# A recurrent attention kernel on one core: float32 rows per segment in DRAM, earlier loads of the first side operands, an order of waits, and a new order of units

## The chip, the core and the metric

The kernel runs on one core of one Trainium2 chip. The metric is the device time of one execution in microseconds. PE is TensorE, DVE VectorE, ACT ScalarE, POOL GpSimd, and SP (SyncE) is the queue from which nearly all DMAs are issued.

## The reference

Two attention branches read the same 2048 x 512 input; a gate mixes them row by row. Cut to what matters:

```python
# branch A: 32 heads of 128; 64 segments of 32 rows; a memory of M = 8 rows
mem = mem0
for s in range(64):
    h = concatenate([mem, x[32 * s:32 * (s + 1)]])        # 40 rows
    q, k, v = h @ Wq, h @ Wk, h @ Wv                      # per head
    p = softmax(where(mask, q @ k.T * E ** -0.5, -1e9))   # memory rows see all, the others are causal
    o = sum_over_heads(p @ v @ Wo)
    mem, out[s] = o[:8], o[8:]                            # the memory goes into the next segment
# branch B: 32 heads of 16; 4 blocks of 512 rows; softmax inside a block, and a running sum
for s in range(4):
    o = sig(beta) * (phi(q) @ Mem) / (phi(q) @ z + 1e-6) + (1 - sig(beta)) * softmax(q @ k.T * D ** -0.5 + mask) @ v
    Mem, z = Mem + phi(k).T @ v, z + sum(phi(k))
b = o @ wo
g = sigmoid((x * gate_w).sum(-1))
return g * a + (1 - g) * b
```

Branch A is a recurrence: segment s + 1 can't begin its products before the eight memory rows of segment s are there.

## The kernel before, in words

**How it is built.** The kernel records operations engine by engine (`Prog`, L79), with what each reads and writes, and then emits each engine's list in the recorded order. `_plan_waits` (L153) decides for which earlier operations each one waits on a semaphore: its dependencies are sorted by age, the youngest first, and those that an earlier wait covers are dropped. `emit` (L192) issues the waits that are left in the list's order. Where an instruction has two, the built program keeps the first of the list on the instruction, and the second becomes an instruction of its own ahead of it.

**Prologue.** 256 KB pieces of x and branch B's weights, then Wk, Wq and Wv in 1 MB pieces and Wo, are loaded while PE projects the first three blocks of branch B (`b_projections`, L650, a list of 52 pieces). Their Q, K and V go to DRAM (`scr_kqd`, `scr_vd`), and `BAttn.load` (L879) brings what one job of branch B's attention needs back: K in four loads of 16 KB for each half G (`KTj`), Q in one of 128 KB (`QTj`), V in one (`Vj`). `build` (L239) asks for the first job's operands after pieces 36 (K, G = 0), 37 (Q), 38 (K, G = 1), 40 and 42 (V).

**The order.** All the rest is cut into units, and `A_ORDER` (L1049) is a written-out list of their names, in which they are recorded. It sets the order on every engine. A `~` behind a name swaps ACT and DVE for the PSUM copies of that unit. Units of segment s:

- `s.K0x s.K0y s.K1x ... s.V1y`: half passes of the projections of the segment's 32 columns (8 of memory, 24 of x), PE, L1266; `Q1x`, `Q1y` are quarters by head, L1492. `k0`, `q0`, `v0` ... copy them out of PSUM (ACT or DVE; those of V are called `Vev`), `TK0`, `TQ0` ... transpose them on DVE.
- `Z` (mask bias), `S` (scores), `X` (exp, ACT), `Y` (mask), `M` (sums), `L` (reciprocal, ACT), `N`, `n` (normalise: DVE, POOL), for two halves of the heads.
- `PV` (values, L1616), `E0` to `E3` (copies to `OT_sb`), `W0` to `W3` (output projection, L1353), `hm` (the memory of the next segment: a transpose, a copy and two additions on DVE, L1653 to L1658, the additions named `hma`, `hmb`, into `xTp`).
- `H` copies the segment's float32 result to `WN` (one buffer of 128 x 256, ACT or DVE), and `ws` stores it to DRAM (`sta`). `H` of the next segment waits until that store has read `WN`.

The last 8 rows of each segment feed no memory. Those of four segments are taken together as a group (`L0.` to `L15.`: projections; `O0.` to `O15.`: their output projection, of which `e` copies to the same `WN`, `olev`, and `s` stores it, `sto`). `T0.` to `T15.` finish a group of 128 rows: `l` loads the float32 rows, `a` adds their two halves on POOL (`asum`), `b` is branch B's output projection, `t` scales that on ACT into `t1_sb` (`t1`, L1453, after `asum` has read that tile), `f` mixes on DVE and stores the output. The last segment's rows go straight from PSUM to the output (`finz`, L1662), with a part `t1z` (ACT, L1458) that stands behind `t1` of group 15.

`bS`, `bE`, `bP`, `bT` are branch B's scores (L923), exponentials (ACT, L944, with a mask on POOL, L950), values (L976) and the rest; `pj`, `pp` project its last block late; `wl` loads a piece of Wo.

**The rows in DRAM.** `scr_aRow` is `[16, 4, 4, 5, 8, 256]`: group, column quarter, segment in the group, 8-row part, row, columns. A segment stores parts 0 to 3 of its place, the left rows part 4 of all four segments. A group's load reads parts 1 to 4 in four DMAs of 128 KB, two into `aF` and two into `t1_sb`:

```python
rows[0:SEG * n, q, :]  <-  aRow[g, 2 * i + q, 0:n, 1:5].rearrange("r o i w -> r (o i) w")   # i, q in 0..1; n = 4, 3 in the last group
```

Each load depends on all of the group's stores. `aF` lives through the whole program; `t1_sb` lies where the prologue's buffers were.

Of the kernel before, what the change touches and what calls it, by code (L numbers as in the profile page):

```python
# [78 lines left out]
class Prog:  # L79
# [73 lines left out]
    def _plan_waits(self):  # L153
# [5 lines left out]
        top = {}  # L159
# [8 lines left out]
        for o in sorted((o for e in self.ENGS for o in self.ops[e] if o.born is not None), key=lambda o: o.born):  # L168
# [70 lines left out]
def build(nc, es, A_x, A_mem0, A_Wq, A_Wk, A_Wv, A_Wo, B_wq, B_wk, B_wv, B_wo, B_beta, gate_w, out, dbg=None):  # L239
# [31 lines left out]
    def alloc(stack, *specs):  # L271
        at, spans = 0, {}
        for name, shape, dt, n in specs:
# [21 lines left out]
          ("WN", [128, 256], F32, 0), ("tt", [128, 2 * C, SEG], F32, 0), ("tu", [128, 2 * C, M], F32, 0), ("aF", [128, DM], F32, 0))  # L295
# [16 lines left out]
          ("oTt", [128, 16, 32], F32, 0), ("t1_sb", [128, DM], F32, 0))  # L312
# [13 lines left out]
    dram("aRow", [NG, 4, 4, 5, 8, 256], F32)  # L326
# [4 lines left out]
    def Rs(name):  # L331
        if name not in R:
            R[name] = Res(name)
            home = v.home(name)
            if home:
# [6 lines left out]
             ("OT", "OT_sb"), ("oTt", "oTt"), ("t1_", "t1_sb"))  # L342
# [47 lines left out]
    for n in range(len(pieces)):  # L390
# [15 lines left out]
        if n in (36, 37, 38, 40, 42):  # L406
            bat.load(0, n // 2 % 2 if n != 37 else 0, "kv"[n // 40] if n != 37 else "q")
# [371 lines left out]
class LateB:  # L779


    def __init__(self, v):
# [4 lines left out]
        self.vst = v.t1_sb[:, :].bitcast(BF16)[:, 0:544].rearrange("p (h w) -> p h w", w=17)  # L787
# [71 lines left out]
class BAttn:  # L859
# [190 lines left out]
    L0.xl 0.Q1x 0.q1x L0.KL1x L0.QL1x bS L0.KL1y bE bE pj L0.KL0x wl pj wl L0.VL0x L0.KL1e~ L0.VL0y L0.VL1x wl pp~ L0.VL0e L0.VL1y L0.VL1e~ 0.TQ1x 0.K0x  # L1050
    0.K0y L0.KL0y 0.K1x L0.QL1y 0.Q1y 0.q1y 0.V0x L0.KL0e~ 0.k0 0.K1y 0.V0y L0.QL0x 0.Q0x L0.QL0y wl pj L0.QL1e 0.TK0 wl pj bE wl 0.Q0y wl L1.xl 0.k1
    0.V1x 0.v0~ 0.q0~ 0.Z1 L0.QL0e~ 0.TK1 0.TQ0 L1.KL0x L1.QL0x 0.qt bE 0.TQ1y L1.KL1x 0.S1 0.S0 L1.KL1y 0.V1y 0.X1 0.X0 0.Y0 L1.KL1e~ 0.M1 L1.KL0y
    L1.QL0y 0.M0 L1.QL1x L1.QL1y L0.VLt pj 0.v1 wl 0.L0 0.N0 0.n0 pp 0.L1 L1.QL1e 1.qt 0.N1 pj bP 0.n1 L1.KL0e~ 0.PV 0.E1 bP 0.E0 0.W0 0.W1 0.E3 0.E2 0.W2
    0.W3 0.hm bS pp 1.Z1 bE L1.QL0e 1.K0x bE 1.Q0x 1.Q1x 1.q1x~ 1.Q0y 0.H bE 1.q0 1.TQ1x 1.K0y 1.Q1y 1.TQ0 1.K1x 0.oL bE 1.K1y 1.k0 1.q1y bP bP 1.k1 1.TK0
    1.S0 1.X0 bS 1.TQ1y 0.ws bE 1.V0x 1.TK1 bE 1.S1 1.Y0 1.V0y 1.M0 1.V1x 1.X1 1.L0 1.M1 1.V1y 1.v0 1.L1 1.n0 1.n1 pj pj 1.N0 1.N1 1.v1~ 1.PV bE pp~ 1.E2~
    1.E0 1.E1~ L1.VL0x 1.W0 1.E3~ bE 1.oL 1.W1 1.W2 1.W3 bP 1.hm 1.H bP bS L1.VL0y bE bE 2.K0x bT 2.K0y L1.VL0e 2.Q0x 2.Q1x bE bE 2.Q0y 2.q1x 2.qt 2.k0~
    2.Q1y 2.TK0 bP bP bS 2.q0~ 2.TQ0 2.q1y~ 2.K1x 2.TQ1y bE 2.K1y bE 2.S0 bE 2.V0x 2.X0 1.ws pj 2.TQ1x pj 2.k1~ bE 2.TK1 2.Z1 2.S1 2.Y0 2.M0 2.V0y bP 2.X1
    2.L0 bP 2.M1 bS pp~ 2.L1 2.V1x 2.n0 2.v0 2.N1 bE 2.N0 2.V1y 2.n1 bE 2.v1 pj bE pj bE 2.PV 2.E0 2.E3 pj 2.E1~ pj 2.W0 2.W1 bT 2.E2 2.W2 bP 2.W3 bP bS
    pp 2.hm bE bE pj pj bE 3.K0x 3.qt 2.H 3.K0y 3.Q0x 3.Q0y 3.k0~ 3.TK0 3.q0~ 3.K1x 3.K1y pp~ 3.Q1y bE 3.TQ0 3.k1 3.q1y~ 3.Z1 3.Q1x 3.S0 3.TK1 3.TQ1y
    3.V1x 3.V1y 3.q1x 3.TQ1x 3.S1 3.X0 3.Y0 2.ws pp 3.M0 3.X1 bS 3.M1 bP 3.L0 3.v1 bP 3.n0 3.V0x 3.V0y L1.VL1x 3.L1 2.oL 3.n1 3.N0 bE bE 3.N1 3.v0 bE  # L1060
    L1.VL1y 3.PV pj 3.E0~ 3.E1~ pj 3.E3 bE L1.VL1e 4.qt 3.W0 3.W1 bP 3.E2 3.W2 bT 3.W3 bS pp bP 3.hm 3.H bE bE 3.oL pj pj 4.Q1x 4.K0x L1.VLt pp bT 4.K0y
# [24 lines left out]
    L4.KL1e~ 13.Q0x 13.Q0y 13.K1x 13.q0~ 13.k0~ 13.K1y 13.TK0 13.TQ0 13.Q1x 13.Q1y 13.k1 13.q1x 13.S0 13.TK1 13.q1y 13.TQ1x 13.V1x 13.V1y 13.TQ1y 13.X0
# [149 lines left out]
def plan_a(v, nseg):  # L1236
# [136 lines left out]
    def ol_units(g):  # L1373
# [96 lines left out]
    def segment(s):  # L1470
# [201 lines left out]
        def w_rows():  # L1672
            rows_out(v.aRow[g, :, r, 0:4], WN[:, :], [rw], Rs("aTd%d" % s), P.group("as%d" % s, "as%d" % (s % 2)), "sta%d" % s)
# [90 lines left out]
```

## Time and profile before

| | us |
|---|---|
| runs: median (lowest, highest) of 3 | 854.94 (851.87, 856.57) |
| profiled execution | 855.72 |
| its span, first to last instruction | 852.7 |
| PE busy | 791.9 (93%) |
| DVE busy | 581.7 (68%) |
| ACT busy | 567.4 (67%) |
| POOL busy | 287.6 (34%) |
| granted PE clock | 0.992 |

The span is what the rows of the trace add up to; 3.0 us of the profiled execution lie outside of it. In rows that say who waited for whom, the numbers are the total in us, how often, and the longest. In rows of the timeline they are the start and the length in us, and in brackets how long the engine had been idle and what ended that. A busy PE is not PE at its peak, since the ends of pipelined products are modelled.

### The profile page before, as it was taken

How to read it: one execution, taken by the hardware profiler on the slowest of the kernel's cores; microseconds unless marked ns; L12 is line 12 of the kernel's file. 1: busy time of each engine (PE TensorE's matmuls, PEld its weight loads, DVE VectorE, ACT ScalarE, POOL GpSimd, SP SyncE). 2: the span in 40 equal slices, each digit the busy share in tenths (PEclk: the TensorE clock that was granted, in tenths of full speed). 3: DMA queues.
4: the chain of work that ended last, by engine and by line, in shares of the span. 5: the costliest groups of instructions: out<-in, count | busy, mean ns of one | idle time of the engine just before them, and what ended most of it. 6: DMA issues, size and time to landing. Idle time of an engine off the chain costs nothing.

```text
span 852.7 us, 51641 instructions
## 1 busy us (share of the span) xinstructions
PE 791.9 (93%) x23291; PEld 490.6 (58%) x23291; DVE 581.7 (68%) x1467; ACT 567.4 (67%) x1370; POOL 287.6 (34%) x728
## 2 busy tenths in 40 slices
PE   9978999999998999999999899999999999999883
PEld 4535556565565656655666566556656555655552
DVE  4535666766778776787778686777776577787543
ACT  5535777866767677776747677686576776885442
POOL 4501333432424333342422334252242342452120
PEclk9989999999999999999999999999999999999998
DMA  9995332122212211212213121112222121211221
GB/s 331 416 364 165 81 100 73 33 64 64 70 41 74 51 56 52 61 41 63 79 30 81 38 67 55 48 44 54 68 73 60 48 58 58 58 32 37 78 81 44
DMA packets 98867, 72.33 MB, mean 85 GB/s; under 512 B 56304, under 2 KB 92760, under 8 KB 97112
## 3 DMA queue, kind: packets, MB, share of 16 engines
q1 hardware_dynamic: 97928, 68.24, 26.7%
q8 instruction: 182, 2.98, 1.5%
q10 hardware_dynamic: 720, 0.80, 0.3%
q14 instruction: 37, 0.30, 0.1%
HBM read 43.43 MB, written 25.58 MB: 81 GB/s over the span
## 4 chain that ended last, share of the span: by engine, by line
PE 68%; DMA 10%; DVE 8%; ACT 6%; issue 3%; POOL 2%; SPq 2%; POOLq 0%; DVEq 0%; ACTq 0%
PE ps L1266 35%; PE ps L1353 12%; PE ps L1492 5%; DMA scr_aRow<-WN 5%; PE ps L1616 2%; PE ps L923 2%; PE ps L976 2%; POOL PT L950 2%; DMA t_sb<-scr_aRow 2%; DMA scr_kqd<-stgk 2%; PE ps L1552 1%; PE ps L1585 1%; DMA QTj<-scr_kqd 1%; ACT R_sb L1595 1%; PE ps L827 1%
## 5 line engine op out<-in xcount | busy, mean ns | idle before, releaser
L944 ACT ACTIVATE PT<-ps 128x512 bf16<-128x512 f32 x320 | 173.5, 602 | 57.2 <-PE ps L923 48.8
L950 POOL TENSOR_SCALAR_AFFINE_SELECT PT<-PT 128x128 bf16<-128x128 bf16 (+2 forms) x320 | 121.1, 378 | 219.1 <-ACT PT L944 200.2
L1266 PE MATMUL ps<-Wv_sb,xTp 128*32 128x512 bf16 x2048 | 144.0, 379 | 3.9 <-ACT WN L374 3.0
L1266 PE MATMUL ps<-Wk_sb,xTp 128*32 128x512 bf16 x2048 | 134.8, 380 | 6.7 <-DVE xTp L1658 2.9
L1353 PE MATMUL ps<-Wo_sb,OT_sb 128*32 128x256 bf16 x4032 | 123.2, 273 | 7.8 <-issue 4.7
L1353 PEld LDWEIGHTS ps<-Wo_sb,OT_sb 128*32 128x32 bf16 x4032 | 102.4, 97 | 29.3 <-ACT OT_sb L374 19.7
L1604 POOL TENSOR_TENSOR P_sb<-P_sb,R_sb 128x64 bf16<-128x64 bf16 x128 | 47.4, 370 | 163.1 <-ACT R_sb L1595 159.9
L1266 PEld LDWEIGHTS ps<-Wk_sb,xTp 128*32 128x32 bf16 x2048 | 56.9, 96 | 58.8 <-ACT PT L944 5.6
L374 ACT ACTIVATE OT_sb<-ps 128x320 bf16<-128x320 f32 x176 | 65.2, 438 | 32.8 <-PE ps L1627 32.2
L374 ACT ACTIVATE QN_sb<-ps 128x256 bf16<-128x256 f32 (+1 forms) x156 | 68.5, 442 | 27.5 <-PE ps L1266 20.9
L374 ACT ACTIVATE KN_sb<-ps 128x512 bf16<-128x512 f32 x97 | 58.1, 600 | 41.7 <-PE ps L1266 40.9
L1266 PE MATMUL ps<-Wq_sb,xTp 128*32 128x512 bf16 x1024 | 71.7, 380 | 3.5 <-DVE xTp L1658 3.2
L1278 DVE STREAM_TRANSPOSE KT_sb<-KN_sb 128x256 f32<-128x256 f32 x128 | 55.7, 436 | 26.9 <-ACT KN_sb L374 24.0
L1278 DVE STREAM_TRANSPOSE QT_sb<-QN_sb 128x128 f32<-128x128 f32 (+1 forms) x192 | 63.4, 337 | 14.2 <-ACT QN_sb L374 12.1
L1492 PE MATMUL ps<-Wq_sb,xTp 128*32 128x256 bf16 x2048 | 71.9, 273 | 0.0
L376 DVE CAST V_sb<-ps 128x512 bf16<-128x512 f32 x83 | 56.9, 688 | 19.6 <-PE ps L1266 17.9
L1653 DVE STREAM_TRANSPOSE tt<-ps 128x256 f32<-128x256 f32 x63 | 28.3, 450 | 56.1 <-PE ps L1353 55.5
L1492 PEld LDWEIGHTS ps<-Wq_sb,xTp 128*32 128x32 bf16 x2048 | 56.5, 97 | 15.9 <-DVE QN_sb L376 0.4
L1566 ACT ACTIVATE P_sb<-ps 128x224 bf16<-128x224 f32 x128 | 45.5, 358 | 29.1 <-PE ps L1557 23.9
L376 DVE CAST OT_sb<-ps 128x320 bf16<-128x320 f32 x80 | 36.5, 486 | 26.6 <-PE ps L1627 26.4
L1266 PEld LDWEIGHTS ps<-Wv_sb,xTp 128*32 128x32 bf16 x2048 | 44.0, 95 | 16.5 <-ACT WN L374 3.7
L1599 DVE TENSOR_TENSOR P_sb<-P_sb,R_sb 128x160 bf16<-128x160 bf16 x128 | 41.5, 336 | 16.1 <-ACT R_sb L1595 15.3
(142 smaller groups left out, 1408.6 us busy)
## 6 DMA issues: line engine op xcount, KB each, us to landing
scr_aRow<-WN SPq DMA_DIRECT2D x79, 128.0 KB, 2.3
Wk_sb<-in_A_Wk_dram SPq DMA_DIRECT2D x4, 1024.0 KB, 9.7
Wq_sb<-in_A_Wq_dram SPq DMA_DIRECT2D x4, 1024.0 KB, 13.6
Wv_sb<-in_A_Wv_dram SPq DMA_DIRECT2D x4, 1024.0 KB, 16.2
Wo_sb<-in_A_Wo_dram SPq DMA_DIRECT2D x8, 512.0 KB, 6.4
scr_vld<-VNL SPq DMA_DIRECT2D x16, 256.0 KB, 2.8
VL<-scr_vld SPq DMA_DIRECT2D x64, 64.0 KB
aF<-scr_aRow SPq DMA_DIRECT2D x30, 128.0 KB
```

The lines of the kernel that those rows point to most:

```text
L374: P.op("act", lambda a: a.activation(dst, src, ACT.Copy), reads=[v.rbank[k] for k in bks], writes=dres, name=name)
L376: P.op("dve", lambda d: d.tensor_copy(dst, src), reads=[v.rbank[k] for k in bks], writes=dres, name=name)
L944: P.op("act", lambda a: a.activation(pt, v.pb[bk], ACT.Exp, scale=v.SCALE_B), reads=[v.rbank[bk]], writes=[rp], name="be%d_%d" % (n, t))
L950: P.op("gp", lambda g: g.affine_select(mv, mv, [[0, len(cut)], [1, 128]], ALU.is_ge, 0.0, base=0, channel_multiplier=-1), reads=[rp], writ ...
L1266: ins = pe.matmul(pb[bk][SEG * j:SEG * (j + 1), :], lhs(c), cols(w, j) if split else w[:, 512 * j:512 * (j + 1)], start=(c == 0), stop=(c ...
L1278: P.op("dve", lambda d: d.transpose(to, src), reads=reads, writes=writes, name=name)
L1353: ins = pe.matmul(pb[bk][SEG * j:SEG * (j + 1), 0:256], lhs(h), Wo_sb[:, h, :].rearrange("p (k q c) -> p q k c", q=2, c=64)[:, j % 2], sta ...
L1492: ins = pe.matmul(pb[bk][SEG * j:SEG * (j + 1), 0:256], lhs(c), cols(w_sb[:, c, 2048 * b + 1024 * half:2048 * b + 1024 * (half + 1)], j), ...
L1566: P.op("act", lambda a: a.activation(P_sb[:, b, :], pb[bk][:, 0:So], ACT.Exp, scale=SCALE), reads=[rbank[bk]], writes=[Rs("Pm%d" % b), Rs( ...
L1599: P.op("dve", lambda d: d.tensor_tensor(wide[b][:, :, 0:L], wide[b][:, :, 0:L], R_sb[:, b, :].rearrange("p (i q) -> p i q", q=L), ALU.mult ...
L1604: P.op(ENG["n"], lambda d: d.tensor_tensor(left, left, grp04(R_sb[:, b, :]), ALU.mult), reads=[Rs("R0_%d" % b)], writes=[Rs("PL%d" % b)], ...
L1653: P.op("dve", lambda d: d.transpose(v.tt[:, :, :].rearrange("p (k n) t -> p k n t", n=2), src), reads=[rbank[wb["bk"]]], writes=[Rs("tt")] ...
```

## The change

1. The DRAM rows are stored per segment, `aTd [64, 128, 256]`, and per group of left rows, `aTl [16, 128, 256]`. A store is the 128 x 256 tile as it is. A group's load becomes eight DMAs (six in the last group): for each segment one of 24 partitions x 4 x 1 KB and one of 8 partitions x 4 x 1 KB. Each depends on its own store alone, and all share one semaphore ring.
2. `aF` and `t1_sb` become one tile `AR [128, 2, 512]`, in the place of `t1_sb`.
3. The first job's K and Q of branch B are asked for after pieces 30, 31 and 32 instead of 36, 37 and 38; V stays.
4. Each operation's waits are sorted once more: on PE first those for operations named `hm...` and `Vev...`, last an engine's wait for itself.
5. `A_ORDER` is a new list of the same units, with the `~` marks set anew. On ACT there are 10 copies more and on DVE 10 fewer.

```diff
@@ _plan_waits
+            o.waits.sort(key=lambda d: 2 if d.eng == o.eng else 0 if o.eng == "pe" and d.name.startswith(("hm", "Vev")) else 1)
             o.known = dict(now)
@@ build
-          ("WN", [128, 256], F32, 0), ("tt", [128, 2 * C, SEG], F32, 0), ("tu", [128, 2 * C, M], F32, 0), ("aF", [128, DM], F32, 0))
+          ("WN", [128, 256], F32, 0), ("tt", [128, 2 * C, SEG], F32, 0), ("tu", [128, 2 * C, M], F32, 0))
-          ("oTt", [128, 16, 32], F32, 0), ("t1_sb", [128, DM], F32, 0))
+          ("oTt", [128, 16, 32], F32, 0), ("AR", [128, 2, DM], F32, 0))
-    dram("aRow", [NG, 4, 4, 5, 8, 256], F32)
+    dram("aTd", [NSEG, 128, 256], F32)
+    dram("aTl", [NG, 128, 256], F32)
-        if n in (36, 37, 38, 40, 42):
-            bat.load(0, n // 2 % 2 if n != 37 else 0, "kv"[n // 40] if n != 37 else "q")
+        if n in (30, 31, 32, 40, 42):
+            bat.load(0, n // 2 % 2 if n > 32 else n // 32, "v" if n > 32 else "kqk"[n - 30])
@@ A_ORDER, its beginning
-    L0.xl 0.Q1x 0.q1x L0.KL1x L0.QL1x bS L0.KL1y bE bE pj L0.KL0x wl pj wl L0.VL0x L0.KL1e~ L0.VL0y L0.VL1x wl pp~ L0.VL0e L0.VL1y L0.VL1e~ 0.TQ1x 0.K0x
+    0.Q1x wl L0.xl 0.q1x L0.KL0x L0.KL1x L0.QL1x L0.KL0y 0.Q1y bS L0.KL1y bE pj L0.KL1e~ pj wl 0.K1x bE L0.VL0x L0.VL0y wl pp~ wl L0.VL1x L0.VL1y L0.VL0e
...
@@ A_ORDER, its end
-    63.Z1 62.hm 62.oL O15.0 T14.a 62.H O15.1 O15.2 63.Q0x 63.K1x O15.3 62.ws 63.Q0y 63.K1y 63.K0x 63.Q1x O15.e 63.q0 63.K0y O15.s 63.k1~ T14.t 63.q1x
-    63.V0x T14.f T15.l 63.TK1 63.TQ1x 63.k0 63.Q1y 63.TK0 63.TQ0 T15.b 63.V1x 63.V0y 63.q1y 63.TQ1y 63.S1 63.v0 63.V1y 63.S0 63.X1 63.M1 63.X0 63.Y0 63.M0
+    62.L1 61.oL 62.V0y 62.n0 62.v0~ 62.n1 62.N0 62.N1 62.PV~ 62.E0 62.W0 T14.l 62.E1~ 62.E3~ 62.E2~ 62.W1 62.oL 62.W2 62.W3 O15.0 62.hm 63.qt O15.1 O15.2
+    63.Q1y O15.3 T14.a 63.K0x~ 62.H 62.ws T14.b O15.e 63.K1x~ 63.Q1x 63.q1y 63.K1y T14.t O15.s 63.k1 T14.f 63.Q0x T15.l 63.Q0y 63.q0 63.TK1 63.q1x 63.TQ1y
...
@@ plan_a: ol_units, tail_units, segment
-            rows_out(v.aRow[g, :, :, 4], v.WN[:, :], [Rs("WN")], Rs("aTl%d" % g), P.group("sl%d" % g, "sl"), "sto%d" % g)
+            rows_out(v.aTl[g], v.WN[:, :], [Rs("WN")], Rs("aTl%d" % g), P.group("sl%d" % g, "sl"), "sto%d" % g)
-            for i, (t, res) in enumerate(((v.aF, "aF"), (t1_sb, "t1_"))):
-                grp = P.group("al%d_%d" % (g, i), "al%d" % i)
-                rows = t[:, :].rearrange("p (q w) -> p q w", q=2)
-                n = 3 if last else 4
-                for q in range(2):
-                    P.dma(grp, lambda sp, i=i, q=q, rows=rows, n=n: sp.dma_start(rows[0:SEG * n, q, :], v.aRow[g, 2 * i + q, 0:n, 1:5].rearrange("r o i w -> r (o i) w")),
-                          reads=[Rs("aTd%d" % (4 * g + r)) for r in range(n)] + [Rs("aTl%d" % g)], writes=[Rs(res)], name="lda%d_%d" % (g, i), scratch=True)
+            grp = P.group("al%d" % g, "al")
+            rows = v.AR[:, :, :].rearrange("p h (q w) -> p (h q) w", q=2)
+            for r in range(3 if last else 4):
+                P.dma(grp, lambda sp, r=r: sp.dma_start(rows[SEG * r:SEG * (r + 1) - M], v.aTd[4 * g + r].rearrange("(k t) w -> t k w", k=4)[M:SEG]),
+                      reads=[Rs("aTd%d" % (4 * g + r))], writes=[Rs("t1_"), Rs("aR")], name="lda%d_%d" % (g, r), scratch=True)
+                P.dma(grp, lambda sp, r=r: sp.dma_start(rows[SEG * (r + 1) - M:SEG * (r + 1)], v.aTl[g].rearrange("(k r i) w -> r i k w", k=4, r=4)[r]),
+                      reads=[Rs("aTl%d" % g)], writes=[Rs("t1_"), Rs("aR")], name="ldb%d_%d" % (g, r), scratch=True)
-            rows_out(v.aRow[g, :, r, 0:4], WN[:, :], [rw], Rs("aTd%d" % s), P.group("as%d" % s, "as%d" % (s % 2)), "sta%d" % s)
+            rows_out(v.aTd[s], WN[:, :], [rw], Rs("aTd%d" % s), P.group("as%d" % s, "as%d" % (s % 2)), "sta%d" % s)
```

`asum` reads the two halves of `AR` in the place of `aF` and `t1_sb`; branch B's late V is staged in `AR`'s first half.

More of the change, by code (lines that the diff above doesn't have):

```diff
@@ L341, in build @@
              ("QT", "QT_sb"), ("VN", "V_sb"), ("Pm", "P_sb"), ("PL", "P_sb"), ("R0", "R_sb"), ("OTL", "OTL"),
-             ("OT", "OT_sb"), ("oTt", "oTt"), ("t1_", "t1_sb"))
+             ("OT", "OT_sb"), ("oTt", "oTt"), ("t1_", "AR"), ("aR", "AR"))
     def late_home(name):
@@ L786, in __init__ @@
         self.work = [("V", t) for t in range(4)] + [(m, f) for f in range(4) for m in "KQ"]
[L787 removed]
+        self.vst = v.AR[:, 0, :].bitcast(BF16)[:, 0:544].rearrange("p (h w) -> p h w", w=17)
         self.kst = v.aTg[:, :, :].rearrange("p c t -> p (c t)")
@@ new lines @@
+    33.K0y 33.Q1y~ 33.Q0y~ 32.oL 33.k0 33.q1y~ 33.TK0 33.Q1x~ bE 32.ws 33.K1x~ O7.e~ 33.K1y~ 33.q0~ 33.q1x O7.s 33.TQ0 bP bP 33.S0 T6.a bS~ 33.TQ1x
+    33.TQ1y 33.k1 33.X0 bE 33.TK1 33.V1x 33.S1 33.Y0 33.V1y~ bE 33.M0 33.X1 33.L0 33.v1 33.V0x~ 33.M1 33.V0y~ L9.QL0x 33.N0 L9.QL0y 33.L1 33.n0 33.v0~
+    33.n1 33.N1 bE 33.PV~ 33.E0 33.E2 bE L9.KL1x 33.W0 33.E1 33.W1 33.E3 33.W2 33.W3 bP 34.qt L9.QL0e bP 33.hm bS 33.H L9.KL1y 33.ws bT bE 34.Q0x bE
+    34.Q0y~ 34.K0x 33.oL 34.q0 bE bE 34.K0y~ 34.k0 34.K1x~ 34.Z1 34.TK0 34.K1y 34.TQ0 34.k1 34.Q1y 34.Q1x 34.q1y 34.TK1 34.q1x 34.TQ1y 34.S0 34.TQ1x
@@ L1230 @@
+    63.V1x 63.V0x 63.K0y 63.TQ1x 63.S1 63.V0y 63.TQ0 63.k0~ T15.b 63.TK0 63.v0 63.V1y 63.S0 63.X1 63.M1 63.X0 63.Y0 63.M0 63.L0 63.v1 63.L1 63.n0 63.N0
+    63.N1 63.n1 63.PV 63.E0 T15.a 63.W0 63.E1~ 63.W1 63.E2 63.E3 T15.t 63.W2 63.W3 63.H T15.f
 """
@@ L1247, in plan_a @@
     OT_sb, OTL, t1_sb, g_sb, omg_sb, out2d, g_out = (
-        v.OT_sb, v.OTL, v.t1_sb, v.g_sb, v.omg_sb, v.out2d, v.g_out)
+        v.OT_sb, v.OTL, v.AR[:, 0, :], v.g_sb, v.omg_sb, v.out2d, v.g_out)
     bat, oTg, aTg = v.bat, v.oTg, v.aTg
```

346 lines of the change are left out of this document (171 added, 175 removed).

## The prediction

> **What bounds the kernel now.** I read the page's header and busy line first, then who PE waited for, then who waited for the float32 rows in DRAM, then the end of the chain.
>
> ```profile
> span 852.7 us, 51641 instructions
> PE 791.9 (93%) x23291; PEld 490.6 (58%) x23291; DVE 581.7 (68%) x1467; ACT 567.4 (67%) x1370; POOL 287.6 (34%) x728
> PE ps L1266 <- DVE xTp L1658: 6.0, 15, 1.4
> PE ps L923 <- DMA QTj<-scr_kqd: 4.3, 1, 4.3
> PE ps L1616 <- DVE P_sb L1599: 4.0, 7, 1.7
> PE ps L1266 <- ACT WN L374: 3.8, 4, 1.9
> PE ps L1616 <- ACT V_sb L374: 3.7, 10, 0.8
> PE ps L1266 <- ACT t_sb L1453: 1.7, 1, 1.7
>   POOL aTg L1422: 29.3, 11
>   ACT WN L374: 20.0, 9
> ```
>
> PE is busy 791.9 of 852.7 us, and the change leaves its 23,291 products as they are. So the time can only come from the other 61 us: PE's waits, the start and the end. The waits fall in three kinds. One is a single long wait in the prologue (`QTj`). Then there are many short ones for the producers of the recurrence: the new memory `xTp`, `P_sb`, `V_sb`. The third comes from the DMA traffic of `scr_aRow`: the last two rows, which are from the view of that tensor, say that POOL stood 29.3 us for its loads and ACT 20.0 us for its stores, and PE felt this as 3.8 us (a bank that the copy to `WN` had not yet freed) and 1.7 us (the bank of `t1`).
>
> The profiled execution took 855.7 us, 3.0 more than its span. The sum is made against 855.7; the median of the runs, 854.9, is 0.8 lower. About 0.5% (4.3 us) is what a measurement of this kernel can tell from no change.
>
> **The DMA layout.** Here are the late end of the chain, the two ACT rows that belong to it, the last product and the last addition, a left-row store, and DMA in two windows (the last two columns are the busy share of 16 engines and GB/s).
>
> ```profile
> 821.83 7.80 DMA scr_aRow<-WN
> 830.12 3.25 DMA scr_aRow<-WN
> 833.81 3.92 DMA scr_aRow<-WN
> 840.06 5.90 DMA t_sb<-scr_aRow
> 846.05 1.29 POOLq L235
> 829.71 0.38 ACT L374 ACTIVATE WN<-ps 128x256 f32<-128x256 f32 x1 [4.15 <-DMA scr_aRow<-WN]
> 833.40 0.38 ACT L374 ACTIVATE WN<-ps 128x256 f32<-128x256 f32 x1 [3.30 <-DMA scr_aRow<-WN]
> 844.07 0.57 PE L1365 MATMUL ps<-Wo_sb,OT_sb 128*32 128x128 bf16 x27 [1.03 <-issue]
> 848.42 0.35 DVE L1662 SCALAR_TENSOR_TENSOR KTL<-ps,g_sb,KTL 128x128 bf16<-128x128 f32 x1 [7.00 <-ACT KTL L1458]
> scr_aRow<-WN SPq DMA_DIRECT2D x1, 128.0 KB, 2.3
> 30.00:56.00 26.00, 20.49 (x240) 11.99 (x237) 9.99 (x23) 11.21 (x22) 6.47 (x31) 0.97 1.04 404
> 841.00:845.00 4.00, 2.20 (x128) 1.85 (x128) 0.42 (x1) 1.02 (x3) 0.00 (x0) 1.00 0.21 71
> ```
>
> While the four last loads ran (841 to 845) the share was 0.21 of 16 engines, about 3, at 71 GB/s, though nothing else was queued; the prologue fills all 16 at 404. The loads' DRAM side has 3 as its outer size there (4 elsewhere). A segment's store, outer size 4, took 3.25 us (830.12); a left-row store of the same 128 KB, outer size 16, took 2.3 (the one at 444.0). So the outer size decides how many engines work, about 24 GB/s each (71 over 3). The new segment store has 128 outside on both sides: it should land in 2.3 us, 1.0 less. The new loads have 24 and 8 outside. At 8 engines and more, the last group's 384 KB need at most 384/(8 x 24) = 2.0 us in place of 5.4. From first issue to landing they took 8.3 us (sum of issue and the 5.90 row); I take 5, between 8.3 (no gain) and 4. What a store queued behind such loads loses (7.80 instead of 3.25 at 821.83) goes too.
>
> The Trainium skill, "DMA: Bandwidth & Descriptors", section "Why a DMA increments its semaphore by 16 and not by 1", says that a copy runs on the largest k up to 16 that divides the slowest dimension of both sides: k = 4 or 3 now, and 16, 12 and 8 after. The trace agrees with the 3.
>
> What this is worth: at the end, the last product is done at 844.07 + 0.57 = 844.6, but the last rows are added only at 848.4, because `t1z` stands in ACT's queue behind `t1_15`, that waits for `asum15` on POOL and this for the loads. With stores and loads 1 to 4 us faster each, the products end last: 848.4 - 844.7 = **-3.7 us**, and 0 if the loads don't gain; I take -3.5. Before that, ACT stood 4.15 and 3.30 us in its queue with segment 63's copies behind it; PE's own waits for `WN` and `t_sb` are 3.8 + 1.7 = 5.5. About two thirds of these go (-3.5), and I add -2.5 for the held ACT queue, of which PE sees only the later parts: **-6 us**, from 0 (new short waits: the new order puts several copies to `WN` within one unit of the store before) to -9. SP issues eight loads a group in place of four; its queue has room, and the loads are wanted microseconds later.
>
> **First side operands.** SP's queue in the prologue, the two landings, and PE:
>
> ```profile
> 41.56 0.43 SPq L527 DMA_DIRECT2D Wv_sb<-in_A_Wv_dram  x1
> 42.04 3.06 SPq L891 DMA_DIRECT2D KTj<-scr_kqd  x4
> 45.15 0.42 SPq L891 DMA_DIRECT2D QTj<-scr_kqd  x1
> 46.11 2.73 SPq L891 DMA_DIRECT2D KTj<-scr_kqd  x4
> QTj<-scr_kqd SPq DMA_DIRECT2D x1, 128.0 KB, 10.9
> Wv_sb<-in_A_Wv_dram SPq DMA_DIRECT2D x1, 1024.0 KB, 13.5
> 50.76 0.60 PE L1266 MATMUL ps<-Wk_sb,xL 128*32 128x512 bf16 x8
> 51.19 0.60 PE L1266 MATMUL ps<-Wq_sb,xL 128*32 128x512 bf16 x8
> 56.09 0.62 PE L923 MATMUL ps<-QTj,KTj 32*128 32x256 bf16 x8 [4.29 <-DMA QTj<-scr_kqd]
> 60.03 2.43 PE L1266 MATMUL ps<-Wv_sb,xL 128*32 128x512 bf16 x32
> ```
>
> The nine loads move ahead of the last two `Wv` pieces, some 8 us up SP's queue, so `QTj` lands near 48 instead of 56. The new order also puts three more half passes of 0.43 us (50.76 to 51.19) ahead of the first `bS`, which so begins near 53 without a wait: -4.3. What is late next is `Wv`: the last piece, issued 41.56, lands near 55. Four half passes now stand between `bS` and the first product with `Wv`, so that product comes at 55 to 56, not 60.03. The 0.25 MB moved ahead of `Wv` cost 0.6 us at 404 GB/s, since the DMA engines are full there. If instead `Wv` lands as much later as its issue moves (3.06 + 0.42 + 2.73 = 6.2 us), the whole gain goes. I take **-3 us**, from -4.3 to 0.
>
> **The order of waits.** Producer and consumer, three pairs:
>
> ```profile
> 315.87 0.38 DVE L1658 TENSOR_TENSOR xTp<-tt,tu 64x32 bf16<-64x32 f32 x2
> 316.31 0.61 PE L1266 MATMUL ps<-Wq_sb,xTp 128*32 128x512 bf16 x8 [0.22 <-DVE xTp L1658]
> 433.91 0.60 DVE L1658 TENSOR_TENSOR xTp<-tt,tu 64x32 bf16<-64x32 f32 x2
> 434.66 0.83 PE L1266 MATMUL ps<-Wq_sb,xTp 128*32 128x512 bf16 x12 [0.19 <-ACT PT L944]
> 631.23 0.58 ACT L374 ACTIVATE V_sb<-ps 128x512 bf16<-128x512 f32 x1
> 631.96 0.38 PE L1616 MATMUL ps<-P_sb,V_sb 32*128 32x40 bf16 x32 [0.33 <-ACT V_sb L374]
> ```
>
> Where the late producer is the product's only wait, the product starts 0.06 us after it (316.25 to 316.31). Where a product has two waits, the built program gives the first of its list to the product and the second to an instruction of its own ahead of it; if the late one is that second, the product starts 0.15 us after it (434.51 to 434.66, 631.81 to 631.96). The new sort puts `hm` and `Vev` first on PE, so they fall on the product: 0.09 us saved each time. I count 52 products in the trace that start 0.14 to 0.15 us after such a second `hm` or `Vev` (two of them shown) and 3 for which the other wait is the late one, which lose 0.09. That is (52 - 3) x 0.09 = 4.4 us, all on the recurrence, where nothing is beside it. The new order will not have the same 52: **-4 us**, from -2 to -5. The same sort puts an engine's wait for itself last in the list; POOL, which always has one, gains or loses 0.1 us at a time away from PE: nothing.
>
> **The new order** moves units without changing them; ten PSUM copies go from DVE to ACT, both about two thirds busy. No row prices it. PE's waits for the three producers above are 6.0 + 4.0 + 3.7 = 13.7 us; a bad order could add most of that again, a good one take a third. In the last segments it holds back less filler for 60 and 62 and more for 63. Adding up the units that the two orders put between the links of the recurrence I find no better cover, rather a little less: **+2 us**, from -5 to +10.
>
> Sum: -3.5 - 6 - 3 - 4 + 2 = -14.5, so 855.7 - 14.5 = 841.2 against the profiled execution; **841 us**.
>
> **Rivals.** *The order eats it* (0.16): cover is lost at +10 to +14, and the `WN` waits come back elsewhere; for it: several copies to `WN` follow a store by one unit; against it: these stores land a microsecond sooner. 841 + 8 to 12 gives about 851. *More is freed* (0.2): ACT's and POOL's holds (20.0 and 29.3 us) delayed the recurrence more than PE's own waits tell; with 8 us more, 833. *Small loads in series* (0.07), the slower side:
>
> ```profile
> 210.41 1.27 POOL L1422 TENSOR_TENSOR aTg<-aF,t_sb 128x512 bf16<-128x512 f32 x1 [6.34 <-DMA t_sb<-scr_aRow]
> KTj<-scr_kqd SPq DMA_DIRECT2D x2, 16.0 KB, 2.2
> ```
>
> If each of the eight loads took its 2.2 us after the one before, a group would need 17.6 us in place of 8.3, and POOL, whose queue holds `asum` ahead of the scores' and values' own work, would stand 9.3 us longer in each group; of the 6.34 us at 210.41 PE felt 1.7, a quarter. 16 x 9.3 x 0.27 = 40 us at most, about 25 with cover: -7 + 2 + 25 gives 876. It decides once a group's loads outlast the units between `l` and `a`, which the new order cuts to one `T1.b` in group 1. Against it: 4 loads of 128 KB shared one stretch at 71 GB/s without gaps. The Trainium skill speaks for it in "DMA: Bandwidth & Descriptors", section "Rules for kernel authors": join small transfers, since under 64 KB one pays mostly overhead, and four of the eight are 32 KB.
>
> **How the numbers follow.** Forecast 836 to 848: 0.57; 833: 0.2; order eats: 0.16, a part of it past 851 to each side; series: 0.07. Faster by over 0.5% means under 850.6: 0.57 + 0.2 + 0.03 = 0.8; slower 0.07 + 0.03 = 0.1; same 0.1. The range from 831 to 853 takes in the first three but for their ends.
>
> **What would show it.** Right: no wait of PE for `QTj`; segment stores landing in 2.3 us; POOL's total for the rows well under 29.3 and ACT's under 10; first products of a segment 0.06 us after `hm`; the last addition right behind the last product. Wrong: PE waiting near 56 for `Wv`; POOL waiting longer ahead of `asum`; PE's waits for `xTp`, `P_sb` and `V_sb` over 14 us together.

## The result, and the profile after

| | before | after |
|---|---|---|
| runs: median (lowest, highest) of 4 each, us | 853.99 (851.87, 856.57) | 841.55 (840.80, 842.46) |
| ratio after / before, 95% interval | | 0.9854 [0.9822, 0.9885] |
| profiled execution, us | 855.72 | 841.06 |
| its span, us | 852.7 | 838.5 |

The change makes the kernel 1.5% faster, 12.4 us by the medians. The forecast was 841 us. Its terms must still be looked at one by one, because a right sum can hold wrong terms, and here it does.

The first lines are the header, the busy line and the chain of the profile after, and then those for whom PE waited longest (in total, how often, the longest, in us).

```profile
span 838.5 us, 51703 instructions
PE 792.9 (95%) x23291; PEld 489.1 (58%) x23291; DVE 575.0 (69%) x1457; ACT 570.1 (68%) x1380; POOL 288.6 (34%) x728
PE 82%; DVE 7%; ACT 5%; issue 3%; DMA 1%; POOL 1%; DVEq 0%; POOLq 0%
PE ps L1357 <- issue: 6.8, 10, 1.0
PE ps L1620 <- DVE P_sb L1603: 3.8, 7, 1.7
PE ps L1270 <- DVE AR L378: 3.3, 1, 3.3
PE ps L1270 <- DVE xTp L1662: 3.1, 7, 1.1
PE ps L1620 <- ACT V_sb L376: 2.4, 6, 0.9
```

PE's work is what it was (792.9 us against 791.9), so the 14.2 us that the span lost were waits, and idle time at the end. The wait for `QTj` (4.3) is gone and so are those for banks held by the copies to `WN` (3.8) and by `t1` (1.7). At the half passes `xTp` fell from 6.0 to 3.1, though the quarters by head now wait 1.5 us for it, which they did not before; `V_sb` fell from 3.7 to 2.4. The largest new line is 3.3 us, once, for a copy into `AR` in the prologue. DMA has 1% of the chain, where it had 10% in the page of before.

Next are the stores and loads of the rows: the group of segment stores, who waited for them (after the median landing in the first row, the columns are total us and times), and a stretch in which the last loads ran, whose last two columns are the busy share of 16 DMA engines and GB/s.

```profile
scr_aTd<-WN SPq DMA_DIRECT2D x63, 128.0 KB, 2.1
  ACT WN L376: 7.6, 3
  DVE WN L378: 0.2, 1
823.50:827.50 4.00, 3.12 (x116) 1.63 (x108) 2.94 (x10) 0.71 (x2) 0.00 (x0) 1.00 0.43 131
```

POOL stood 29.3 us for the loads before; among those who waited for the new tensors it does not appear. ACT's 20.0 us became 7.6. While the last loads ran, the DMA engines moved 131 GB/s, a store of the output among it, where the old loads had 71. Worked out from the landings in the traces, a group's loads took 9.1 us from the first issue to the last landing before (median of the 16 groups; 8.2 in the last) and take 5.2 now (4.1 in the last). SP issues a group's loads nearly one behind the other in both kernels (2.2 to 4.4 us from the first to the last), so this is not the work of loads that could start earlier than others.

The end of the trace after:

```profile
817.57 3.33 DMA scr_aTd<-WN
820.92 0.38 ACT L376 ACTIVATE WN<-ps 128x256 f32<-128x256 f32 x1 [3.38 <-DMA scr_aTd<-WN]
829.85 1.26 POOL L1426 TENSOR_TENSOR aTg<-AR 96x512 bf16<-96x512 f32 x1 [0.17 <-POOL P_sb L1608]
830.67 3.25 PE L1369 MATMUL ps<-Wo_sb,OT_sb 128*32 128x128 bf16 x128 [0.55 <-ACT OT_sb L376]
833.97 0.35 DVE L1666 SCALAR_TENSOR_TENSOR KTL<-ps,g_sb,KTL 128x128 bf16<-128x128 f32 x1 [3.29 <-PE ps L1369]
```

`asum15` (829.85) no longer waits for a DMA, only for POOL's own operation before it. The last product ends at 833.92 and the last addition begins at 833.97. Before, 3.8 us lay between them.

The prologue after, where PE's largest new wait stands:

```profile
52.98 2.70 SPq L665 DMA_DIRECT2D scr_vd<-V  x4
54.38 0.40 PE L925 MATMUL ps<-QTj,KTj 32*128 32x256 bf16 x8 [0.51 <-issue]
56.79 1.04 PE L1270 MATMUL ps<-Wv_sb,xL 128*32 128x512 bf16 x16
60.07 0.24 POOL L847 MEMSET AR<- 128x32 bf16 x1 [3.24 <-DMA scr_vd<-V]
60.34 0.69 DVE L378 CAST AR<-ps 128x512 bf16<-128x512 f32 x1 [3.47 <-POOL AR L847]
61.09 1.52 PE L1270 MATMUL ps<-Wv_sb,xL 128*32 128x512 bf16 x16 [3.27 <-DVE AR L378]
```

The first scores (54.38) wait for no load, and the first product with `Wv` (56.79) doesn't either. But branch B's late V projection is copied into `AR`, and that memory held V of the prologue. POOL's preparing memset waits until the last prologue store of V, issued from 52.98 on, has read it. The copy, the PSUM bank that it frees, and PE's next product then all wait, 3.27 us.

Last, the order of waits: a pair of the recurrence in the trace after.

```profile
335.40 0.38 DVE L1662 TENSOR_TENSOR xTp<-tt,tu 64x32 bf16<-64x32 f32 x2
335.84 0.55 PEld L1270 LDWEIGHTS ps<-Wk_sb,xTp 128*32 128x32 bf16 x16 [0.40 <-DVE xTp L1662]
335.84 1.05 PE L1270 MATMUL ps<-Wk_sb,xTp 128*32 128x512 bf16 x16
```

This product has two waits, and it starts 0.06 us after the late one (335.78 to 335.84). Of the products that a late `hm` or `Vev` releases, some 80 start so now, and two at most are slower; before, some 55 (32 of `hm`, 23 of `Vev`) started 0.14 to 0.15 us after it.

Where the time came from can be read by setting the two traces side by side at the last output-projection product of each segment, and at the last addition. The numbers are worked out from the traces, each kernel's minus before's, in us; the kernels of the other columns come below.

| at the end of segment | after | sort alone | rows alone | early loads alone | order alone | after, late loads |
|---|---|---|---|---|---|---|
| 0 | -1.7 | -1.3 | -1.2 | +0.4 | -1.7 | -2.5 |
| 10 | -1.2 | -3.7 | -2.0 | +0.4 | -0.5 | -2.6 |
| 11 | -3.0 | -3.9 | -3.9 | -0.4 | -2.4 | -4.6 |
| 32 | -4.6 | -2.3 | -2.0 | +0.3 | -0.4 | -5.4 |
| 33 | -6.6 | -3.2 | -3.5 | +0.1 | +1.5 | -7.5 |
| 58 | -7.5 | -2.8 | -0.4 | +0.7 | +4.0 | -6.4 |
| 60 | -9.8 | -3.1 | -2.8 | +0.3 | +1.9 | -8.7 |
| 63 | -10.7 | -3.4 | -5.7 | +0.6 | +3.9 | -8.8 |
| last addition | -14.4 | -2.9 | -9.4 | +1.0 | +0.1 | -12.6 |

Two executions of the kernel after differ by 0.1 us at segment 0 and by up to 1.4 us later (segments 44 to 46), so a single value tells less than a step. The change comes in steps: -1.8 at segment 11 and -2.0 at segment 33, -2.3 in segments 59 and 60, and -3.7 behind the last product.

### The profile page after: what moved, and what is told of

It is laid out like the page before. It is cut to its first block, busy times and chain, and to the rows that moved or that the text cites. A ratio compares the mean times of both kernels' runs of the same rounds, so it can differ in the third digit from the quotient of the medians.

```text
span 838.5 us, 51703 instructions
## 1 busy us (share of the span) xinstructions
PE 792.9 (95%) x23291; PEld 489.1 (58%) x23291; DVE 575.0 (69%) x1457; ACT 570.1 (68%) x1380; POOL 288.6 (34%) x728
## 4 chain that ended last, share of the span: by engine, by line
PE 82%; DVE 7%; ACT 5%; issue 3%; DMA 1%; POOL 1%; DVEq 0%; POOLq 0%
PE ps L1270 39%; PE ps L1357 15%; PE ps L1496 6%; PE ps L1620 3%; PE ps L691 3%; PE ps L925 3%; PE ps L978 2%; PE ps L1556 2%; PE ps L1589 2%; PE ps L1439 2%; ACT PT L946 1%; PE ps L710 1%; ACT R_sb L1599 1%; PE ps L829 1%; DVE oTt L1002 1%
## 5 line engine op out<-in xcount | busy, mean ns | idle before, releaser
L1608 POOL TENSOR_TENSOR P_sb<-P_sb,R_sb 128x64 bf16<-128x64 bf16 x128 | 49.4, 386 | 161.2 <-ACT R_sb L1599 155.6
L376 ACT ACTIVATE KN_sb<-ps 128x512 bf16<-128x512 f32 x103 | 61.9, 604 | 40.2 <-PE ps L1270 39.2
L376 ACT ACTIVATE QN_sb<-ps 128x256 bf16<-128x256 f32 (+1 forms) x153 | 67.5, 446 | 23.2 <-PE ps L1270 20.4
## 6 DMA issues: line engine op xcount, KB each, us to landing
Wq_sb<-in_A_Wq_dram SPq DMA_DIRECT2D x4, 1024.0 KB, 12.6
```

The source lines that it names most:

```text
L376: P.op("act", lambda a: a.activation(dst, src, ACT.Copy), reads=[v.rbank[k] for k in bks], writes=dres, name=name)
L1608: P.op(ENG["n"], lambda d: d.tensor_tensor(left, left, grp04(R_sb[:, b, :]), ALU.mult), reads=[Rs("R0_%d" % b)], writes=[Rs("PL%d" % b)], ...
```

## The experiments

All ratios are to runs of the kernel before on the same chip, with the 95% interval; 0.001 is 0.85 us. One kernel profiled once has a span that can lie some us from its median, so sizes come from the ratios and places from the traces. One is the changed kernel again; four kernels do one part of the change alone; four undo one part of it; three try what these left open.

| kernel | ratio | gain, us | span |
|---|---|---|---|
| after, again | 0.9850 [0.9821, 0.9880] | 12.8 | 838.5 |
| sort alone | 0.9946 [0.9920, 0.9973] | 4.6 | 849.8 |
| rows alone | 0.9881 [0.9841, 0.9920] | 10.2 | 843.6 |
| early loads alone | 0.9978 [0.9951, 1.0005] | 1.9 | 853.7 |
| order alone | 0.9957 [0.9927, 0.9986] | 3.7 | 852.9 |
| after without the sort | 0.9890 [0.9860, 0.9919] | 9.4 | 842.4 |
| after with the old rows | 0.9935 [0.9911, 0.9958] | 5.6 | 848.3 |
| after with late loads | 0.9859 [0.9833, 0.9885] | 12.0 | 840.4 |
| after with the old order | 0.9844 [0.9816, 0.9871] | 13.3 | 838.6 |
| after, slow segment stores | 0.9848 [0.9817, 0.9879] | 13.0 | 838.1 |
| after, `AR` moved | 0.9822 [0.9791, 0.9853] | 15.2 | 837.6 |
| after, `AR` moved, late loads | 0.9824 [0.9798, 0.9850] | 15.0 | 834.5 |

### After, run again

> The changed kernel again, as the yardstick beside the next ones: 841.5 (840 to 843).

The ratio 0.9850 repeats the first 0.9854, and the last addition is 14.44 us earlier than before's in this trace too (14.45 in the first).

### The sort alone

```diff
@@ before, _plan_waits
+            o.waits.sort(key=lambda d: 2 if d.eng == o.eng else 0 if o.eng == "pe" and d.name.startswith(("hm", "Vev")) else 1)
```

> The kernel before with only the sort of the waits. By the prediction's term: 4 us less, 850 (849 to 852), since some 49 products start 0.09 us sooner, all on the recurrence. By the rival that the saved 0.09 us only meets the next wait (the segment-by-segment difference of the two traces has no steady slope): within 1 us of the kernel before, while the products still start 0.06 us after the memory.

It gains 4.6 us by the ratio, [2.3, 6.8], and POOL's holds stay:

```profile
POOL aTg L1423 <- DMA t_sb<-scr_aRow: 28.9, 11, 6.5
ACT WN L375 <- DMA scr_aRow<-WN: 20.0, 9, 4.1
```

So the gain is that of the waits by themselves. Where it arises is less clear: if 49 products save 0.09 us each, the lead should grow evenly, but the trace is 3.7 us ahead at segment 10 and 2.9 at the end. The kernel after without the sort, below, shows a more even growth.

### The rows alone

```diff
@@ before, with the new tensors, store and load lines and AR; the old order, the old waits, the late first loads
-    dram("aRow", [NG, 4, 4, 5, 8, 256], F32)
+    dram("aTd", [NSEG, 128, 256], F32)
+    dram("aTl", [NG, 128, 256], F32)
```

> The kernel before with only the rows in DRAM per segment (stores, loads, the tile AR), old order, old loads, no sort. By the prediction: 9.5 us less (3.5 at the end, 6 before it), 844 to 846; steps of 1.5 to 2 us in segments 11 and 33 and some 2 us in 59 to 63. By the rival that the new order gives the gain: 2 to 4 us less at most, 850 to 852, only at the end.

It gains 10.2 us, [6.8, 13.6], the largest part. Who waited for the rows, and PE's old wait:

```profile
ACT WN L375 <- DMA scr_aTd<-WN: 8.9, 3, 4.0
POOL aTg L1423 <- issue: 2.4, 1, 2.4
POOL aTg L1423 <- ACT OT_sb L375: 1.4, 1, 1.4
PE ps L924 <- DMA QTj<-scr_kqd: 4.2, 1, 4.2
```

With the order unchanged POOL's 29.3 us are some 3.8 in two stops, and ACT's 20.0 us are 8.9. The profile puts the two stops of POOL down to something else, but in both `asum` starts 0.1 us after the last load of its group has landed (worked out from the landings), so they are still waits for the rows. A group's loads take 5.3 us from the first issue to the last landing (median), much as in after. The steps in the table above stand where the holds stood: at 11, at 33, from 59 on, and 3.7 us at the end.

### The early loads alone

```diff
@@ before, build
-        if n in (36, 37, 38, 40, 42):
-            bat.load(0, n // 2 % 2 if n != 37 else 0, "kv"[n // 40] if n != 37 else "q")
+        if n in (30, 31, 32, 40, 42):
+            bat.load(0, n // 2 % 2 if n > 32 else n // 32, "v" if n > 32 else "kqk"[n - 30])
```

> The kernel before with only the first job's K and Q asked for earlier. By the prediction: 3 us less, 851. By the rival that a copy which waits for the last V store of the prologue takes the place of the wait (the changed kernel shows PE standing 3.3 us for it at 61): 0 to 1 us less.

The ratio leaves a gain open, 1.9 us, [-0.4, 4.2]. The trace does not show it: segment 0 ends 0.4 us later than before. PE's prologue:

```profile
51.95 0.40 PE L923 MATMUL ps<-QTj,KTj 32*128 32x256 bf16 x8
55.92 1.91 PE L1266 MATMUL ps<-Wv_sb,xL 128*32 128x512 bf16 x32 [1.34 <-DMA Wv_sb<-in_A_Wv_dram]
61.06 1.72 PE L1266 MATMUL ps<-Wk_sb,xTp 128*32 128x512 bf16 x16 [3.23 <-DVE t_sb L376]
```

The first scores start at 51.95 without a wait, 4.1 us sooner than before. PE then gives 1.34 us back to `Wv` and 3.23 us to the copy of V into `t_sb`, whose memory is the same reused place as `AR`'s. Before, both had been done by the time PE came, because it had stood for `QTj`.

### The new order alone

```diff
@@ before
-A_ORDER = """ (old list)
+A_ORDER = """ (new list)
```

> The kernel before with only the new order. By the prediction: 2 us more, 856, from 5 less to 10 more. By the rival that the new order gives the gain: 6 us less or more, under 848.

It is faster by 3.7 us, [1.2, 6.2]. The waits for the old rows, a wait of PE, and the last addition:

```profile
POOL aTg L1424 <- DMA t_sb<-scr_aRow: 20.7, 10, 3.2
ACT WN L374 <- DMA scr_aRow<-WN: 4.4, 2, 3.3
PE ps L1554 <- DVE QT_sb L1280: 3.8, 3, 2.6
848.56 0.35 DVE L1664 SCALAR_TENSOR_TENSOR KTL<-ps,g_sb,KTL 128x128 bf16<-128x128 f32 x1 [3.96 <-PE ps L1367]
```

The order alone takes ACT's hold from 20.0 to 4.4 us and POOL's from 29.3 to 20.7: it places the copies and `asum` where the DMAs are mostly done. Part of what the rows cure, it cures too. Its price shows in the third row, a new wait for `QT_sb`. In the trace it loses 3.1 us between segments 32 and 36. The last row shows that the order alone also closes the gap of 3.8 us behind the last product, with the old rows: the last loads are issued 10.9 us before the end of the last product, where they were issued 6.9 us before it, so `asum15` and `t1z` are done in time. This one profiled execution ended level with before (+0.1), at a granted clock of 0.988 against 0.992 and with PE busy for 796.6 us against 791.9. So the trace shows places of gain and loss, but not where the 3.7 us of the ratio come from.

### After without the sort

```diff
@@ after, _plan_waits
-            o.waits.sort(key=lambda d: 2 if d.eng == o.eng else 0 if o.eng == "pe" and d.name.startswith(("hm", "Vev")) else 1)
```

> The changed kernel without the sort of the waits. If the sort is worth the same in the new order as in the old (4.6 us alone): 846. If the new order was drawn for the sort and lost its worth elsewhere, or the sort only pays in the old order: within 1.5 us of the changed kernel.

0.9890 against 0.9850 for after on the same chip: the sort is worth 3.4 us in the new company (medians 845.67 and 842.66; last additions 3.9 us apart). Here the lag behind after grows over the kernel, from nothing at segment 5 and 0.8 us at segment 10 to 3.2 at 32 and 4.1 at 58, as many small losses would have it. The waits of PE that it shortens:

```profile
PE ps L1269 <- DVE xTp L1661: 3.9, 10, 1.1
PE ps L1619 <- ACT V_sb L375: 3.3, 8, 1.0
```

### After with the old rows

```diff
@@ after, with the old tensor, store and load lines, aF and t1_sb
-    dram("aTd", [NSEG, 128, 256], F32)
-    dram("aTl", [NG, 128, 256], F32)
+    dram("aRow", [NG, 4, 4, 5, 8, 256], F32)
```

> The changed kernel with the rows in DRAM as before (stores and loads on 3 to 4 DMA engines, two tiles). If the rows are worth in the new order what they are in the old (10 us alone): 851 to 852. If the new order already holds the stores and loads apart (the order alone gained 3.6 us by its runs, and the four parts alone add up to 20 us against 12.5 together): 846 to 848.

0.9935 against 0.9850: the rows are worth 7.2 us in company, against 10.2 alone; the intervals do not tell the two apart. Less is what one would expect, since the order has taken a part of the holds already, and of the gap behind the last product only 0.9 us is left for the rows to close. POOL's hold here:

```profile
POOL aTg L1425 <- DMA t_sb<-scr_aRow: 20.9, 10, 3.2
```

### After with slow segment stores

The prediction credited both the stores and the loads. This kernel gives the stores their old outer size of 4, by 1 KB of unused space behind every 32 rows, and leaves the loads as they are.

```diff
-    dram("aTd", [NSEG, 128, 256], F32)
+    dram("aTd", [NSEG, 4, 33, 256], F32)
-            rows_out(v.aTd[s], ...
+            rows_out(v.aTd[s, :, 0:SEG], ...
-            ... v.aTd[4 * g + r].rearrange("(k t) w -> t k w", k=4)[M:SEG]
+            ... v.aTd[4 * g + r].rearrange("k t w -> t k w")[M:SEG]
```

> The changed kernel with 1 KB left free behind every 32 rows of a segment in DRAM, so that the segment stores have 4 as their outer size again; the loads keep theirs. If the outer size sets the engines: these stores land in 3.2 us instead of 2.1, ACT waits longer for WN, and the time is 1 to 3 us over the changed kernel (843 to 845), the end staying as it is. If the layout's size or alignment mattered and not the outer size: landings of 2.1 us and no change.

The stores did become slow: by their semaphores they land in 3.29 us (median) in place of 2.07. One of them in the chain, and who waited for them:

```profile
817.43 3.26 DMA scr_aTd<-WN
  ACT WN L376: 6.1, 3
  DVE WN L378: 0.8, 2
```

The time did not change (0.9848 against 0.9850, spans of 838.1 and 838.5), nor did ACT's holds grow (6.1 against 7.6). The intervals, 0.003 to each side, would not show a loss of 1 or 2 us by themselves. But no run shows that a store's 1.2 us are worth anything here. The Trainium skill, "DMA: Bandwidth & Descriptors", section "Why a DMA increments its semaphore by 16 and not by 1", gives 4 engines to an outer size of 4 and 16 to 128; the two landings agree with it, but nobody waits for that speed here. By elimination the gain is that of the loads, and of the stores no longer queued behind slow loads. The landings fit this: the slowest segment store takes 4.8 us here, with slow stores beside fast loads, and took 8.6 in before. No run has slow loads beside fast stores.

### After with `AR` moved

`AR` and `V_sb` are allotted in other places, so that the memset of 60.07 writes to memory that no late prologue store reads.

```diff
@@ after, in_a
-  ... ("LN_sb", ...), ("KTL0", ...
+  ... ("LN_sb", ...), ("AR", [128, 2, DM], F32, 0), ("V_sb", [128, 2, 512], BF16, 0), ("KTL0", ...
```

> The changed kernel with the tile AR (and V_sb) laid over an earlier part of the prologue's buffers, so that branch B's late V need not wait for the prologue's last V store. If that wait (3.3 us of PE near 61) is what ate the gain of the earlier loads: no such wait, and 838 to 840. If segment 0 is held by something else in the prologue (Wv or the DMA engines): the wait turns up elsewhere before 70 us and the time stays at 841 to 842.

The wait is gone, which confirms its cause:

```profile
56.96 0.24 POOL L847 MEMSET AR<- 128x32 bf16 x1
57.23 0.69 DVE L378 CAST AR<-ps 128x512 bf16<-128x512 f32 x1 [0.29 <-POOL AR L847]
PE ps L1357 <- issue: 8.3, 13, 1.0
```

Segment 0 ends 4.7 us earlier than in the kernel before, 2.9 us ahead of after's. At the end of segment 63 the lead over after is 0.9 us; the third row shows 1.5 us more of "issue" waits than after has, the rest I can't name. 0.9822 [0.9791, 0.9853] is the lowest ratio of all, but its interval holds after's.

### After with late loads, with `AR` in place and moved

```diff
@@ after (first kernel), after with AR moved (second kernel), build
-        if n in (30, 31, 32, 40, 42):
+        if n in (36, 37, 38, 40, 42):
```

With `AR` in its place:

> The changed kernel with the first job's K and Q asked for late, as before the change. If the copy that waits for the prologue's last V store sets segment 0 either way: PE stands some 3 us for QTj near 55 and no longer for the copy, and the time is that of the changed kernel, ratio 0.983 to 0.987. If the earlier loads are worth the prediction's 3 us: ratio 0.989.

0.9859: 0.8 us from after's 0.9850, far within the interval. The wait that comes back:

```profile
55.84 0.40 PE L925 MATMUL ps<-QTj,KTj 32*128 32x256 bf16 x8 [3.23 <-DMA QTj<-scr_kqd]
```

In its place the wait for the copy into `AR` is gone (PE's products with `Wv` run from 59.34 without a stop), and segment 0 ends 0.8 us earlier than after's. With `AR` moved:

> The version with AR laid elsewhere, with the first job's K and Q asked for late again, as before the change. If the earlier loads pay once the wait for the prologue's last V store is gone: PE stands some 3 us for QTj near 55 and the time is 2 to 3 us over the version with early loads (842 to 843). If not: within 1 us of it (840 to 841).

0.9824 against 0.9822 with early loads. PE's waits show the old one, and few "issue" stops:

```profile
PE ps L1357 <- issue: 3.3, 5, 1.5
PE ps L925 <- DMA QTj<-scr_kqd: 3.0, 1, 3.0
```

Here nothing takes the place of the `QTj` wait when the loads are early, and indeed segment 0 of the kernel with early loads is 3.4 us ahead. By segment 20 the lead is 0.5 us, and at the last addition the kernel with early loads is 3.1 us behind in the profiled executions. Why the lead is lost stays open. So does another thing: moving `AR` gains 2.4 us with early loads and 3.0 us with late ones by the ratios, and with late loads there was no wait for the copy into `AR` to take away. The intervals overlap in both pairs, so the move may also be worth less.

### After with the old order

```diff
@@ after
-A_ORDER = """ (new list)
+A_ORDER = """ (old list)
```

> The changed kernel with the old order of units. By the prediction's term for the order (2 us more with the new one): 840. If the new order is worth in this company what it is worth alone (3.6 us less): 845. If it is worth nothing beside faster rows: 841 to 843.

0.9844 against 0.9850: the new order costs 0.5 us here, which can't be told from nothing, nor from the +2 of the forecast. One hold is left that the new order avoids:

```profile
POOL aTg L1424 <- DMA AR<-scr_aTl: 5.4, 2, 4.1
```

POOL stands 5.4 us for the loads here and not at all in after; ACT stands 7.7 us for the stores of both kinds, against 7.6. With the rows stored the new way there is little left for the order to avoid, and the time shows nothing of it.

## Why the prediction was right, and which of its steps were not

The sum was -14.5 against the profiled execution; the profiled executions differ by 14.7 and the medians by 12.4. Of its five terms:

- **End, -3.5: right in size.** -3.7 in the table, with the rows alone and in after. The way was the foreseen one: `asum15` no longer waits for loads, so `t1z` is done before the last product. The group's loads that were taken as 5 us for this took 4.1. What the prediction did not see is that the new order closes the same gap without the rows, all of it alone and all but 0.9 us in after with the old rows. So it can be booked to either part, but only once.
- **Rows before the end, -6: right in size, with a reason that fell.** Rows alone gain 10.2 in all, which is 6.5 besides the end (9.5 was predicted for both). The step that failed is what the store's landing in 2.3 us is worth: the landing came (2.1), but making it 3.29 again costs nothing that the runs show. What paid, by elimination, is the load side. POOL's 29.3 us went to 3.8 with the rows alone and to no wait in after, and the stores that stood behind four slow loads (7.80 us in the trace of before) don't any more.
- **First side operands, -3: wrong in its way.** No gain is shown: 1.9 [-0.4, 4.2] alone and 0.8 in company. The ratios do not exclude 3, but the gain is eaten where it arises, for segment 0 ends 0.4 us later with the early loads alone, and 0.8 us later in after than with late loads. "What is late next is `Wv`" is the failed step. In the early loads' kernel `Wv` took 1.34 us, and in after nothing; in both the larger wait, 3.2 us, was that for the V copy into `t_sb` or `AR`, whose memory is reused from the prologue. The prediction looked at what the next products read, and not at who still had to free their bank. Even where that wait was taken away, the 3.4 us at segment 0 did not reach the end.
- **Order of waits, -4: right.** 4.6 alone, 3.4 when left out, and nearly all products behind a late `hm` or `Vev` start at 0.06 us, as the 49 x 0.09 had it.
- **The new order, +2: wrong in its sign alone, near enough in company.** Alone it gained 3.7, with shorter holds on the old rows and no gap at the end; how much of the 3.7 each gave is not shown. In company it costs 0.5, and +2 is within what the runs leave open. The step that failed is "no row prices it": the rows of ACT's and POOL's holds and of the last addition bore on it, because the order decides how far a copy or an `asum` stands behind its DMA.

So the sum was right partly by luck, because errors offset each other: by the ratios in company the loads gain 0.8 where 3 were forecast, and the order costs 0.5 where 2 were. The gains of the four parts alone add up to 20.4 us, and the change gains 12.8. The rows and the order overlap (the order takes ACT's 20.0 us hold to 4.4, the rows take it to 8.9, and both close the gap of 3.8 us at the end; each can be taken only once). The predicted terms were sized as if they were independent; only because the order was given no gain was nothing counted twice.

The rivals: *small loads in series* is refuted, a group's loads take 5.2 us in after and not 17.6, and POOL waits for none of them. The Trainium skill's advice against transfers under 64 KB ("DMA: Bandwidth & Descriptors", section "Rules for kernel authors") did not decide here: eight loads of 96 and 32 KB hold up nobody in after, where four of 128 KB held POOL for 29.3 us in before. *The order eats it* is refuted by the kernel with the old order, *more is freed* by the ratio.

## What to carry to other kernels

When a wait is taken away, ask not only what the next instructions read but who must free the banks and buffers that they write; memory reused from an earlier stage was the answer here, and moving one tile told. Look for the speed of a transfer on the side where somebody waits: the wide loads paid here, and the fast stores showed no gain. Where an instruction has two waits, let the one that comes last be its own; that alone was worth half a per cent of this kernel.

## What the runs showed of the hardware beyond that

- An early lead on PE need not last. With `AR` moved, 3.4 us at segment 0 were 0.5 us at segment 20, with the same order on every engine behind it.
- SP issued the DMAs faster whose two sides have the same shape. Loads into the half tiles before, and into `AR` after (in ns: lowest, median, highest):

```profile
L1418 SPq DMA_DIRECT2D t_sb<-scr_aRow x32: 500/540/879, 202.3 to 840.1; - x32
```

```profile
L1420 SPq DMA_DIRECT2D AR<-scr_aTd x63: 290/299/2007, 195.9 to 824.8; - x63
L1375 SPq DMA_DIRECT2D scr_aTd<-WN x63: 319/422/1507, 85.9 to 817.6; - x63
```

  With the slow stores' padded rows, whose DRAM side is 4 x 32 rows against 128 partitions, the same store takes longer again:

```profile
L1375 SPq DMA_DIRECT2D scr_aTd<-WN x63: 502/547/617, 85.4 to 817.4; - x63
```

  It is not the number of DMA engines: the left-row stores of before, with an outer size of 16 against 128 partitions, took 0.57 us to issue (median), and the new loads of 8 rows 0.31. That the shapes are the cause is only argued from these pairs.
- PE has short stops in the output projection that the profile puts down to nothing ("issue"): 3.3 us in 5 stops in the kernel with `AR` moved and late loads, 8.3 us in 13 in the one with early loads. They differ from kernel to kernel without any part of the change that would explain them, and are as large as the smaller terms here. That is why -3 and +2 can be told from nothing only at the place where they arise.
